# A decode step with cached attention and a gated MLP: whole heads of K and V as 64 KB rows in three slots

## The chip, the cores and the metric

The kernel runs on one core of a Trainium2 chip. The metric is the device time of one execution in microseconds, taken as the median of three runs.

## What is computed

One token (x, 576 wide) goes through a layer norm. Its result xn feeds two branches, and both are added to x:

```python
xn = layernorm(x)
q = (xn @ wq).reshape(32 heads, 128)
scores = einsum("hd,hkd->hk", q, k_cache) * 128**-0.5      # 16384 keys a head
o = einsum("hk,hkd->hd", softmax(scores), v_cache)
h = gelu_tanh(xn @ w_gate) * (xn @ w_up)                   # 4608 wide
out = x + o.reshape(4096) @ wo + h @ w_down
```

All data are float32. The caches hold 32 heads x 16384 x 128 each, 268 MB for K and as much for V. The weights are 9.4 MB (wq, wo) and 10.6 MB (gate, up, down). Everything is read once, so 588 MB cross from HBM into SBUF.

## The kernel before

**Slots.** All large loads go through one pool of five slots of 128 partitions x 32 KB (`SLOTS`, L42, `slot` L58). They are issued by SP, in the order of the program, on one queue; a load waits until the slot it was given is free. A slot is given out as it comes free, not in turn.

**Tiles.** A head has 16384 keys. They are cut into two tiles of 128 partitions x 64 keys (`R = 64`, `C = 2`), so a tile is 4 MB with one contiguous row of 32 KB a partition. There are T = 64 tiles of K and 64 of V. The loop at L254 runs over t: it loads K tile t and V tile t - 3 (`LAG`), computes the scores of K tile t (`qk`) and the weighted sum of V tile t - 3 (`pv`). So softmax of a head lies between them, written out in three parts (`softmax_a`, `_b`, `_c`, L200 to L217) and placed between the blocks by hand.

**Scores.** `qk` (L184) takes 16 keys at a time: VectorE multiplies the block in place by q, which stands in all 128 partitions (L191), then sums ten of the sixteen products (L196), and ScalarE sums the other six by an activation with accumulation (L195).

**PV.** TensorE multiplies four columns of the exponentials with four keys of V, 512 columns at a time (L226), into one of two PSUM banks `PO`. In rows 32q to 32q + 3 of the bank only the four diagonal blocks are wanted. `out_a` (L237) copies the bank to SBUF by ScalarE; `out_b` (L241) picks the diagonal with four matmuls against `sel`; `norm` (L231) sums the exponentials over partitions and inverts; `out_c` (L248) scales and puts the head's 128 outputs in a column of `oall`.

**q.** wq comes in two loads of 2048 columns, 8 KB pieces (L61, L68), with its last 64 rows as a 1 MB load `qt`. At L112 TensorE computes q with xn spread over 128 columns, so that each of the eight results stands in all partitions, 512 columns each, and ScalarE copies it to SBUF.

**Gate and up.** They come in six loads of 1536 columns (6 KB pieces) at t = 1, 3, ..., 11 (`ffn_load` L127), go through TensorE in four column groups (`ffn_mm` L134), are copied by ScalarE (`ffn_copy` L147) and spread over partitions by four small DMAs of POOL (L151). `ffn_act` (L155) computes gelu(gate) x up.

**The end.** After the loop, w_down comes in three loads and wo in loads of 12, 12, 6 and 2 rows a partition. The last of these is cut by partitions into pieces of 8, 4, 2, 1, 112 and 1 (`LAST`, L35). Each row of a weight is two matmuls of 288 columns into `acc` (`add_out`, L294), in four row groups. `oall` is transposed (L315) and its rows are spread by a small DMA into `oT` (L319). Before the last two rows the two upper groups are merged into the lower ones (L337 to L340); the sum with x (L342) and the store (L343) end the kernel.

What a reader may not see from the words is how V's matmul and its column groups are addressed:

```python
for n in range(i * SUB, (i + 1) * SUB, 4):
    k = c * R + n
    q = 32 * (k // 4 % 4)
    nc.tensor.matmul(OP[h][q : q + 4, :], PE_[h][:, k : k + 4], vt[:, n * DH : (n + 4) * DH], ...)
```

The order of the code is not quite the order of execution: a scheduler works at compile time through the program, and on each engine an instruction that it takes to be ready may go ahead of earlier ones that are not. Each engine then runs its list in that fixed order. The memsets of L322 and L336, for instance, run in the first microseconds.

Of the kernel before, what the change touches and what calls it, by code (L numbers as in the profile page):

```python
# [16 lines left out]
R = 64  # L17
C = SK // (P * R)
T = H * C
LAG = 3  # L20
# [3 lines left out]
SLOTS = 5  # L24
DJ = 4
# [4 lines left out]
QS = 2048  # L30
FS = 1536
FQ = FS // 4
FT = FS // P
WO_T = H * DH // P
LAST = (8, 4, 2, 1, 112, 1)  # L35
# [3 lines left out]
def kernel(ctx: ExitStack, tc: tile.TileContext, x, k_cache, v_cache, wq, wo, wg, wu, wd, out):  # L39
# [3 lines left out]
    spool = ctx.enter_context(tc.tile_pool(name="spool", bufs=3))  # L43
    ps_acc = ctx.enter_context(tc.tile_pool(name="ps_acc", bufs=1, space=bass.MemoryType.PSUM))
    ps_big = ctx.enter_context(tc.tile_pool(name="ps_big", bufs=2, space=bass.MemoryType.PSUM))
# [3 lines left out]
    kv = k_cache.rearrange("b h (c p n) d -> (b h c) p (n d)", p=P, n=R)  # L49
    vv = v_cache.rearrange("b h (c p n) d -> (b h c) p (n d)", p=P, n=R)  # L50
    xf = x.rearrange("b s d -> (b s) d")
    of = out.rearrange("b s d -> (b s) d")
    wmain = {n: w[:DM].rearrange("(p j) f -> p j f", j=DJ) for n, w in (("q", wq), ("g", wg), ("u", wu))}
    wqt = wq[DM:].rearrange("d (s f) -> (d s) f", s=2)
    wov = wo.rearrange("(p t) f -> p t f", t=WO_T)
    wdv = wd.rearrange("(s p t) f -> s p t f", p=P, t=FT)
# [4 lines left out]
    def load_w(n, lo, size):  # L61
        t = slot()
        nc.sync.dma_start(t[:, : DJ * size].rearrange("p (j f) -> p j f", j=DJ), wmain[n][:, :, lo : lo + size])  # L63
        return t

    qt = cpool.tile([P, QS], F32, name="qt")
    nc.sync.dma_start(qt, wqt)
    wq_t = [load_w("q", lo, QS) for lo in range(0, H * DH, QS)]  # L68
# [24 lines left out]
    xn = cpool.tile([1, D], F32, name="xn")  # L93
    nc.vector.tensor_scalar(xn, xrow, mv[:, 0:1], rstd, op0=ALU.subtract, op1=ALU.mult)
    px = ps_s.tile([P, 512], F32, tag="sm", name="px")
    xm = xn[:, :DM].rearrange("o (p j) -> o j p", j=DJ)
# [3 lines left out]
    nc.vector.tensor_copy(xd, xn[:, DM:].unsqueeze(2).to_broadcast([1, D - DM, 2]))  # L100
# [3 lines left out]
    xnb = cpool.tile([P, DJ, P], F32, name="xnb")  # L104
    nc.vector.tensor_copy(xnb, xp[:, :DJ].unsqueeze(2).to_broadcast([P, DJ, P]))
    xt = cpool.tile([P, 2], F32, name="xt")
    nc.vector.tensor_scalar(xt, par, xp[:, DJ:], None, op0=ALU.mult)
    xtb = cpool.tile([P, 2, P], F32, name="xtb")
    nc.vector.tensor_copy(xtb, xt.unsqueeze(2).to_broadcast([P, 2, P]))

    Q = {}
    for s, w in enumerate(wq_t):  # L112
        wv = w.rearrange("p (j f) -> p j f", j=DJ)
        for g in range(QS // 512):
            pq = ps_big.tile([P, 512], F32, tag="pb", name="pq")
            for j in range(DJ):
                nc.tensor.matmul(pq, xnb[:, j, :], wv[:, j, g * 512 : (g + 1) * 512], start=j == 0, stop=False)  # L117
            nc.tensor.matmul(pq, xtb[:, s, :], qt[:, g * 512 : (g + 1) * 512], start=False, stop=True)  # L118
            qs = cpool.tile([P, 4, DH], F32, name=f"q{s}{g}")
            nc.scalar.activation(qs.rearrange("p a d -> p (a d)"), pq, AF.Copy)  # L120
            for i in range(4):
                Q[(s * 4 + g) * 4 + i] = qs[:, i : i + 1, :]

    gu = cpool.tile([P, 2, DF // P], F32, name="gu")
    FW = {}

    def ffn_load(which, s):  # L127
        t = FW[which, s] = load_w("gu"[which], s * FS, FS)
        w = (wg, wu)[which]
        src = bass.AP(tensor=w.tensor, offset=w.offset + DM * DF + s * FS,  # L130
                      ap=[[DF, D - DM], [FS // 2, 2], [1, FS // 2]])
        nc.sync.dma_start(t[:, DJ * FS : DJ * FS + FS // 2], src)

    def ffn_mm(which, s):  # L134
        t = FW.pop((which, s))
        pg = ps_big.tile([P, 512], F32, tag="pb", name="pg")
        for j in range(DJ + 1):
            for q in range(4):
                if j < DJ:
                    lhs, rhs = xnb[:, j, :32], t[:, j * FS + q * FQ : j * FS + (q + 1) * FQ]  # L140
                else:
                    o = DJ * FS + (q % 2) * FQ
                    lhs, rhs = xtb[:, q // 2, :32], t[:, o : o + FQ]
                nc.tensor.matmul(pg[32 * q : 32 * q + 32, :FQ], lhs, rhs, start=j == 0, stop=j == DJ)  # L144
        return pg

    def ffn_copy(pg, which, s):  # L147
        gc = spool.tile([P, FQ], F32, name="gc", bufs=1)
        nc.scalar.activation(gc, pg[:, :FQ], AF.Copy)
        for q in range(4):  # L150
            nc.gpsimd.dma_start(gu[32 * q : 32 * q + 32, which, s * FT : (s + 1) * FT], gc[32 * q : 32 * q + 1, :])  # L151

    hT = cpool.tile([P, DF // P], F32, name="hT")

    def ffn_act():  # L155
        g, u = gu[:, 0], gu[:, 1]
        t1 = cpool.tile([P, DF // P], F32, name="t1")
# [3 lines left out]
        th = cpool.tile([P, DF // P], F32, name="th")  # L161
        nc.scalar.activation(th, t1, AF.Tanh, scale=0.7978845608028654)
        t2 = cpool.tile([P, DF // P], F32, name="t2")
        nc.vector.scalar_tensor_tensor(t2, th, 1.0, g, op0=ALU.add, op1=ALU.mult)
# [207 lines left out]
```

## Time and profile before

| what | value |
|---|---|
| median of 3 runs | 1396.49 us (1396.14 to 1397.85) |
| the profiled execution | 1396.48 us, of which its span is 1394.7 us |
| HBM read | 587.60 MB, 421 GB/s over the span |
| K loads | 64 of 4096 KB, 43.0 us from issue to landing (median) |
| V loads | 64 of 4096 KB, 34.6 us |
| DMA packets | 25618, of them 24692 on SP's queue |

The times in the profile are of one execution, measured by the hardware. The busy time of an engine is the sum of its instructions. A line number such as L191 is a line of the kernel before. The chain that ended last is followed back from the last instruction to whatever released each step. The granted clock of TensorE is a share of its full speed.

### The profile page before, as it was taken

The page shows a single profiled execution, that of the slowest core. Times are in us where ns is not written, and L with a number is a line of the kernel's source. Part 1 is how long each engine was busy: PE and PEld are TensorE (multiplying, and loading weights), DVE is VectorE, ACT ScalarE, POOL GpSimd, SP SyncE. Part 2 cuts the span into 40 slices and gives each one's busy share as a digit, 9 for nine tenths or more (in the row PEclk, how much of TensorE's full clock was granted, in tenths as well). Part 3 has the DMA queues.
Part 4 walks back from the last instruction along what each step waited for, and adds up shares of the span by engine and source line. Part 5 has one row for each costly group of instructions (what it writes and reads, how often), then busy time and mean ns, then how long its engine had stood idle before and what let it go on. Part 6 is the DMA issues. An engine that isn't in the chain of part 4 may idle for free.

```text
span 1394.7 us, 10849 instructions
## 1 busy us (share of the span) xinstructions
PE 527.9 (38%) x3071; PEld 151.4 (11%) x3071; DVE 956.3 (69%) x634; ACT 536.1 (38%) x3251; POOL 14.2 (1%) x33
## 2 busy tenths in 40 slices
PE   6634234344234323342243323332333233332575
PEld 3211001011001000000011000100011001100121
DVE  1977565739877877778777877787777777787500
ACT  0644333325443444344344434444434433443300
POOL 0000000000000000000000000000000000000000
PEclk9866667565665665656656566665666666656677
DMA  9999999999999999999999999999999999999993
GB/s 406 422 426 431 422 432 428 419 438 429 428 432 435 425 432 434 429 430 435 431 428 433 430 432 430 432 430 431 432 432 430 430 433 430 431 432 430 430 428 124
DMA packets 25618, 588.36 MB, mean 422 GB/s; under 512 B 3267, under 2 KB 3285, under 8 KB 7254
## 3 DMA queue, kind: packets, MB, share of 16 engines
q1 hardware_dynamic: 24692, 587.61, 98.4%
q8 instruction: 24, 0.39, 0.1%
q14 instruction: 36, 0.29, 0.1%
q0 software_dynamic: 864, 0.06, 0.0%
q10 hardware_dynamic: 2, 0.00, 0.0%
HBM read 587.60 MB, written 0.00 MB: 421 GB/s over the span
## 4 chain that ended last, share of the span: by engine, by line
DMA 72%; DVE 20%; PE 7%; issue 1%; POOL 0%; SPq 0%; ACT 0%; DVEq 0%
DMA slot<-in_A_k_cache_dram 34%; DMA slot<-in_A_v_cache_dram 34%; DVE slot L191 12%; DVE s L196 7%; PE po L226 5%; DMA slot<-in_A_wo_dram 3%; DMA gu<-gc 2%; PE pg L144 1%; PE acc L297 1%; POOL gu L151 0%; PE pt L206 0%; DVE pm L202 0%; PE pb L212 0%; PE pl L233 0%; SPq L63 0%
## 5 line engine op out<-in xcount | busy, mean ns | idle before, releaser
L191 DVE TENSOR_TENSOR slot<-slot,q 128x2048 f32<-128x2048 f32 x256 | 574.5, 2286 | 259.4 <-DMA slot<-in_A_k_cache_dram 259.3
L226 PE MATMUL po<-slot,pe 128*4 128x512 f32 x2048 | 372.0, 893 | 758.1 <-DMA slot<-in_A_v_cache_dram 758.1
L195 ACT ACTIVATE jk<-slot 128x128 f32<-128x128 f32 x1536 | 453.2, 296 | 521.7 <-DVE slot L191 518.5
L196 DVE TENSOR_REDUCE s<-slot 128x10 f32<-128x1280 f32 x256 | 367.7, 1478 | 0.0
L195 ACT ACTIVATION_READ_ACCUMULATOR jk<-slot 128x1 f32 x1536 | 286.8, 187 | 0.0
L226 PEld LDWEIGHTS po<-slot,pe 128*4 128x4 f32 x2048 | 60.2, 111 | 1015.7 <-DMA slot<-in_A_v_cache_dram 749.6
L245 PE MATMUL pc<-sel,o 128*128 128x1 f32 x256 | 35.3, 259 | 39.6 <-ACT o L239 39.6
L239 ACT ACTIVATE o<-po 128x512 f32<-128x512 f32 x32 | 19.0, 595 | 78.5 <-PE po L226 78.5
L214 ACT ACTIVATE nb<-pb 128x1 f32<-128x1 f32 x32 | 5.5, 171 | 95.6 <-PE pb L212 95.6
L337 DVE COPY part<-acc 64x288 f32<-64x288 f32 x1 | 0.5, 461 | 60.7 <-PE acc L297 60.7
L245 PEld LDWEIGHTS pc<-sel,o 128*128 128x128 f32 x256 | 32.6, 199 | 71.2 <-ACT o L239 71.2
L117 PE MATMUL pq<-slot,xnb 128*128 128x512 f32 x64 | 31.6, 641 | 7.9 <-DMA slot<-in_A_wq_dram 7.9
L235 DVE RECIPROCAL rl<-pl 128x1 f32<-128x1 f32 x32 | 5.4, 169 | 38.2 <-PE pl L233 38.2
L210 DVE TENSOR_REDUCE nm<-pt 1x1 f32<-1x128 f32 x32 | 8.9, 278 | 30.3 <-PE pt L206 30.3
L249 ACT ACTIVATE oall<-pc,rl 128x1 f32<-128x1 f32 x32 | 8.4, 261 | 38.2 <-PE pc L245 38.2
L144 PE MATMUL pg<-slot,xnb 128*32 128x384 f32 x192 | 21.0, 588 | 0.9 <-DMA slot<-in_B_w_up_dram 0.6
L120 ACT ACTIVATE q<-pq 128x512 f32<-128x512 f32 x8 | 4.8, 597 | 38.9 <-PE pq L118 38.9
L212 PE MATMUL pb<-nm,ones 1*128 1x1 f32 x64 | 12.0, 255 | 14.6 <-DVE nm L210 14.6
L297 PE MATMUL acc<-slot,oT 128*1 128x288 f32 x128 | 12.9, 559 | 9.8 <-DMA slot<-in_A_wo_dram 9.8
L206 PE MATMUL pt<-ident,pm 128*1 128x128 f32 x32 | 8.9, 280 | 20.0 <-DVE pm L202 19.8
L117 PEld LDWEIGHTS pq<-slot,xnb 128*128 128x128 f32 x64 | 13.2, 208 | 24.5 <-issue 24.5
L297 PE MATMUL acc<-slot,hT 128*1 128x288 f32 x144 | 12.5, 510 | 6.4 <-DMA slot<-in_B_w_down_dram 6.4
(60 smaller groups left out, 131.3 us busy)
## 6 DMA issues: line engine op xcount, KB each, us to landing
slot<-in_A_k_cache_dram SPq DMA_DIRECT2D x64, 4096.0 KB, 43.0
slot<-in_A_v_cache_dram SPq DMA_DIRECT2D x64, 4096.0 KB, 34.6
slot<-in_B_w_down_dram SPq DMA_DIRECT2D x3, 3456.0 KB, 38.0
slot<-in_B_w_gate_dram SPq DMA_DIRECT2D x3, 3072.0 KB, 43.9
slot<-in_B_w_up_dram SPq DMA_DIRECT2D x3, 3072.0 KB
slot<-in_A_wq_dram SPq DMA_DIRECT2D x2, 4096.0 KB, 14.4
slot<-in_A_wo_dram SPq DMA_DIRECT2D x2, 3456.0 KB
slot<-in_A_wo_dram SPq DMA_DIRECT2D x1, 1728.0 KB, 33.4
```

The source lines that it names most:

```text
L117: nc.tensor.matmul(pq, xnb[:, j, :], wv[:, j, g * 512 : (g + 1) * 512], start=j == 0, stop=False)
L144: nc.tensor.matmul(pg[32 * q : 32 * q + 32, :FQ], lhs, rhs, start=j == 0, stop=j == DJ)
L191: nc.vector.tensor_mul(blk, blk, Q[h].to_broadcast([P, SUB, DH]))
L195: nc.scalar.activation(jk, blk[:, n, :], AF.Copy, accum_out=S[h][:, o + n : o + n + 1])
L196: nc.vector.tensor_reduce(S[h][:, o : o + nv], blk[:, :nv, :], axis=AX.X, op=ALU.add)
L206: nc.tensor.transpose(PT[h][:1, :P], PM.pop(h), ident)
L210: nc.vector.tensor_reduce(nm, PT.pop(h)[:1, :P], axis=AX.X, op=ALU.max, negate=True)
L212: nc.tensor.matmul(pb[:, :1], ones[:1, :], nm, start=True, stop=True)
L226: nc.tensor.matmul(OP[h][q : q + 4, :], PE_[h][:, k : k + 4], vt[:, n * DH : (n + 4) * DH], start=k < 16, stop=k >= C * R - 16)
L239: nc.scalar.activation(OS[h], OP.pop(h), AF.Copy)
L245: nc.tensor.matmul(PC[h][:, :1], o4[:, j * DH : (j + 1) * DH], sel[:, j : j + 1], start=j == 0, stop=j == 3)
L297: nc.tensor.matmul(acc[q : q + 1, :HALF], lhs, w[:, i * HALF : (i + 1) * HALF], start=q not in seen, stop=last)
```

## The change

- **Rows and slots.** A tile is now a whole head: 128 partitions x 128 keys, 8 MB, one row of 64 KB a partition (`R = 128`). There are three slots of 64 KB a partition. The loop runs over heads without a lag: load K and V of head h, eight blocks of scores, softmax, PV.
- **Weights first.** wq is one load of 128 rows of 64 KB. Gate and up are loaded whole before the first head: three of their four rows a partition in a slot each, the fourth row and the last 64 weight rows in a slot `mix` that also holds wq's last rows. The copy of gate's and of up's result lies in the same slot as its weights, until four small DMAs of POOL have spread it.
- **q.** It is computed in four column groups with xn spread over 32 columns, one copy of 128 x 1024; a head's q is then spread over the partitions by a matmul against ones, a head ahead (`q_spread`).
- **PV's diagonal.** VectorE multiplies the PSUM bank in place by `sel` and sums the four blocks; TensorE then sums over partitions with one matmul against ones.
- **Normalisation.** The sums of the exponentials are kept for all heads (`lsum`) and summed over partitions, inverted and multiplied in at the end.
- **The end.** w_down comes as 28 and 8 rows a partition, wo as 20, 6, 3, 2 and 1 rows, all over 128 partitions; the merge comes before row 26.

The core of the diff:

```diff
-R = 64
+R = SK // P
-SLOTS = 5
+SLOTS = 3
-LAST = (8, 4, 2, 1, 112, 1)
+WD_PIECES = (28, 8)
+WO_PIECES = (20, 6, 3, 2, 1)
+MERGE = 26
...
-    kv = k_cache.rearrange("b h (c p n) d -> (b h c) p (n d)", p=P, n=R)
+    kv = k_cache.rearrange("b h (p n) d -> (b h) p (n d)", p=P)
...
+    mix, wq_t = slot(), slot()
...
+    tails = {"q": part_of_mix(wtail["q"])}
+    load(wq_t, wmain["q"])
+    row3 = {}
+    for n in "gu":
+        row3[n] = part_of_mix(wmain[n][:, ROW3:])
+        tails[n] = part_of_mix(wtail[n])
...
+    def q_spread(h):
+        r = 32 * (h // (H // 4))
+        lo = h % (H // 4) * DH
+        pq = ps_s.tile([P, 512], F32, tag="sm", name="pq")
+        nc.tensor.matmul(pq[:, :DH], ones[r : r + 1, :], qrow[r : r + 1, lo : lo + DH], start=True, stop=True)
+        Q[h] = spool.tile([P, 1, DH], F32, name="qs")
+        nc.scalar.activation(Q[h][:, 0, :], pq[:, :DH], AF.Copy)
...
+    def ffn(which):
+        n = "gu"[which]
+        t = slot()
+        w = load(t[:, :ROW3], wmain[n][:, :ROW3])
+        gc = t[:, ROW3 : ROW3 + FG]
+        steps = [(3, row3[n]), (DJ, tails[n])] + [(j, w[:, j * DF : (j + 1) * DF]) for j in range(3)]
+        pg = project(steps, FG, FB)
+        nc.scalar.activation(gc.rearrange("p (b f) -> p b f", f=FB), pg, AF.Copy)
         for q in range(4):
-            nc.gpsimd.dma_start(gu[32 * q : 32 * q + 32, which, s * FT : (s + 1) * FT], gc[32 * q : 32 * q + 1, :])
+            nc.gpsimd.dma_start(gu[32 * q : 32 * q + 32, which, :], gc[32 * q : 32 * q + 1, :])
...
     def out_a(h):
-        OS[h] = spool.tile([P, 512], F32, name="o4", bufs=1)
-        nc.scalar.activation(OS[h], OP.pop(h), AF.Copy)
+        o4 = PO[h % 2].rearrange("p (r d) -> p r d", d=DH)
+        nc.vector.tensor_mul(o4, o4, sel.unsqueeze(2).to_broadcast([P, 4, DH]))
+        OM[h] = spool.tile([P, DH], F32, name="om")
+        nc.vector.tensor_reduce(OM[h], o4.rearrange("p r d -> p d r"), axis=AX.X, op=ALU.add)
...
+    q_spread(0)
+    for h in range(H):
+        KT[h] = load(slot(), kv[h])
+        VT[h] = load(slot(), vv[h])
         for i in range(NSUB):
+            qk(h, i)
+            if h == 0 and i == 3:
+                ffn_act()
+            if h > 0 and i == 3:
+                out_a(h - 1)
+                out_b(h - 1)
+        KT.pop(h)
+        softmax(h)
+        if h + 1 < H:
+            q_spread(h + 1)
+        pv(h)
...
+    out_a(H - 1)
+    out_b(H - 1)
+    for j, w in enumerate(wd_rows):
+        add_out(j % 2, hT[:, j : j + 1], w)
+
+    pl = ps_s.tile([P, 512], F32, tag="sm", name="pl")
+    nc.tensor.matmul(pl[:, :H], ones, lsum, start=True, stop=True)
+    rl = cpool.tile([P, H], F32, name="rl")
+    nc.vector.reciprocal(rl, pl[:, :H])
+    on = cpool.tile([P, H], F32, name="on")
+    nc.vector.tensor_mul(on, oall, rl)
     po = ps_s.tile([P, 512], F32, tag="sm", name="pot")
-    nc.tensor.transpose(po[:H, :P], oall, ident)
+    nc.tensor.transpose(po[:H, :P], on, ident)
```

`project` runs a list of weight rows through TensorE, for each row two or three blocks of columns in four column groups. `part_of_mix` loads a piece into the next free columns of `mix`.

More of the change, by code (lines that the diff above doesn't have):

```diff
@@ L59, in slot, with load @@
         return slots.tile([P, R * DH], F32, tag="s", name="slot")
[L61 to L68, printed above, removed]
+    def load(dst, src):
+        nc.sync.dma_start(dst, src)
+        return dst
+    mix, wq_t = slot(), slot()
@@ L124 @@
[L124 to L145, printed above, removed]
@@ L299, in add_out @@
             seen.add(q)
[L301 to L312 removed]
+    wd0, wd1, wo1 = slot(), slot(), slot()
@@ new lines @@
+    a, b = WD_PIECES
+    n0 = WO_PIECES[0]
+    load(wd0[:, : a * D], wdv[:, : a * D])
+    load(wd1[:, : b * D], wdv[:, a * D :])
+    load(wd1[:, b * D : (b + n0) * D], wov[:, : n0 * D])
+    lo = n0
+    for n in WO_PIECES[1:]:
+        load(wo1[:, (lo - n0) * D : (lo + n - n0) * D], wov[:, lo * D : (lo + n) * D])
+        lo += n
+    wd_rows = [wd0[:, j * D : (j + 1) * D] for j in range(a)] + [wd1[:, j * D : (j + 1) * D] for j in range(b)]
+    wo_rows = [wd1[:, (b + j) * D : (b + j + 1) * D] for j in range(n0)]
```

245 lines of the change are left out of this document (87 added, 158 removed).

## The prediction

> **What bounds the kernel now.** First the page: where the engines are busy, then what the DMA queues did, then the chain that ended last.
>
> ```profile
> PE 527.9 (38%) x3071; PEld 151.4 (11%) x3071; DVE 956.3 (69%) x634; ACT 536.1 (38%) x3251; POOL 14.2 (1%) x33
> ...
> GB/s 406 422 426 431 422 432 428 419 438 429 428 432 435 425 432 434 429 430 435 431 428 433 430 432 430 432 430 431 432 432 430 430 433 430 431 432 430 430 428 124
> DMA packets 25618, 588.36 MB, mean 422 GB/s; under 512 B 3267, under 2 KB 3285, under 8 KB 7254
> ...
> q1 hardware_dynamic: 24692, 587.61, 98.4%
> ...
> DMA 72%; DVE 20%; PE 7%; issue 1%; POOL 0%; SPq 0%; ACT 0%; DVEq 0%
> ```
>
> No engine is over 69%; the one queue that SP feeds keeps the sixteen DMA engines 98.4% busy, and 72% of the chain is DMA. The rate is flat but for the last slice. So I read the rate by stage (columns: stretch, its length, busy time and count of PE, PEld, DVE, ACT, POOL, then granted clock, DMA share, GB/s).
>
> ```profile
> 10.00:20.00 10.00, 4.23 (x5) 1.85 (x6) 0.00 (x0) 0.00 (x0) 0.00 (x0) 1.00 1.01 424
> 2.00:100.00 98.00, 55.45 (x194) 23.63 (x198) 63.26 (x53) 37.69 (x210) 3.10 (x6) 0.81 1.00 424
> 100.00:350.00 250.00, 96.84 (x597) 27.73 (x589) 161.87 (x107) 91.38 (x554) 9.79 (x20) 0.65 1.01 429
> 350.00:700.00 350.00, 116.06 (x669) 30.75 (x673) 265.24 (x171) 146.32 (x901) 0.00 (x0) 0.64 1.00 431
> 1050.00:1364.00 314.00, 123.06 (x750) 32.55 (x750) 202.01 (x131) 114.05 (x692) 0.56 (x1) 0.65 1.00 431
> 1364.00:1368.00 4.00, 3.09 (x48) 1.14 (x48) 0.00 (x0) 0.00 (x0) 0.00 (x0) 1.00 0.96 312
> 1368.00:1372.00 4.00, 0.00 (x0) 0.00 (x0) 0.00 (x0) 0.00 (x0) 0.00 (x0) 0.71 0.57 209
> 1376.00:1380.00 4.00, 4.00 (x36) 1.19 (x32) 0.00 (x0) 0.00 (x0) 0.00 (x0) 0.51 0.06 28
> 1384.00:1388.00 4.00, 4.00 (x48) 1.52 (x44) 0.00 (x0) 0.00 (x0) 0.00 (x0) 0.66 0.08 28
> 1388.00:1392.00 4.00, 2.86 (x36) 0.79 (x24) 0.91 (x2) 0.00 (x0) 0.00 (x0) 1.00 0.00 1
> ```
>
> From 350 us to 1364 us the DMA share is 1.00 at 431 GB/s: nothing but fewer or cheaper packets can shorten that stretch. The last rows say more. After 1372 us the share is 0.06, which is 1/16: **one engine** works alone at 28 GB/s for some 15 us. The kernel ends when this late engine ends, not when the average one does. Is its lateness made by the eight-four-two-one-row cuts of the last load? The chain of waits and the issues on SP's queue answer that (start, length, what).
>
> ```profile
> 1346.43 36.53 DMA slot<-in_A_wo_dram
> 1383.00 6.28 PE acc L297 x72
> 1389.30 0.47 DVE part L337
> 1390.47 0.99 PE acc L297 x8
> 1391.49 0.45 DVE x L342
> ...
> 1361.01 3.83 SPq L305 DMA_DIRECT2D slot<-in_A_wo_dram  x5
> ```
>
> The load issued at 1346.43 lands only at 1383.00, and the cut pieces were issued behind it, at 1361.01 and after. So the engine was already late before the cuts: every engine carries the same bytes, one of them loses time along the way, and the end is its end. I take this lag as unchanged: every engine still carries a sixteenth of the same bytes, and the work of the other engines beside it hardly changes.
>
> The profiled execution took 1396.48 us, 1.8 us more than its span, and stands at the median of the runs (1396.49). A change under 0.2% (2.8 us) counts as none, about what a measurement of this kernel can tell.
>
> **What the change takes off the DMA.** *K and V.* Rows of 8 KB (wq, 10 to 20 us) ran at 424 GB/s, rows of 32 KB at 431. Per engine that is 8192 x 16 / 424 = 309.1 ns and 32768 x 16 / 431 = 1216.4 ns a row, so a byte costs 0.0369 ns and a row 6.7 ns beside its bytes. A head's K and V now take one row of 64 KB a partition: 8192 rows fewer, 512 an engine, 512 x 6.7 ns = **3.4 us less**. Bounds: no gain, if a row goes out in two pieces; and a loss of 20.6 us, if long rows run at the 424 of the slowest steady row (536.9 MB at 424 instead of 431). I take 3.4, since the 32 KB rows are nearest.
>
> The Trainium skill speaks against it: "DMA: Bandwidth & Descriptors", section "Latency and other measured facts", has copies slowed by row pitches at large powers of two (207 GB/s at 512 KiB, 164 at 2 MiB). By it a doubled pitch could cost rate; no run here shows that so far, and what it would cost by this trace is the first rival below.
>
> *wq, gate, up.* wq goes from 8 KB to 64 KB rows, gate and up from 6 KB to 54 KB and 18 KB. Against 431, the first 98 us lost 98 x 7/431 = 1.6 us and the next 250 us 250 x 2/431 = 1.2 us, and these hold all loads of small rows: **2.8 us less** (bounds 0 and 2.8). *The last rows.* The cuts give the lowest engines a row of the 8, 4 and 2 pieces besides 7 of the 112, ten rows for eight; without them 2 x 4.6 KB at 28 GB/s, **0.3 us less** (0 to 0.5). Together 6.5.
>
> **What hides beside the DMA.** Durations from the groups (busy, mean ns of one):
>
> ```profile
> L191 DVE TENSOR_TENSOR slot<-slot,q 128x2048 f32<-128x2048 f32 x256 | 574.5, 2286 | 259.4 <-DMA slot<-in_A_k_cache_dram 259.3
> L195 ACT ACTIVATE jk<-slot 128x128 f32<-128x128 f32 x1536 | 453.2, 296 | 521.7 <-DVE slot L191 518.5
> L196 DVE TENSOR_REDUCE s<-slot 128x10 f32<-128x1280 f32 x256 | 367.7, 1478 | 0.0
> L245 PE MATMUL pc<-sel,o 128*128 128x1 f32 x256 | 35.3, 259 | 39.6 <-ACT o L239 39.6
> L239 ACT ACTIVATE o<-po 128x512 f32<-128x512 f32 x32 | 19.0, 595 | 78.5 <-PE po L226 78.5
> L337 DVE COPY part<-acc 64x288 f32<-64x288 f32 x1 | 0.5, 461 | 60.7 <-PE acc L297 60.7
> L202 DVE TENSOR_REDUCE pm<-s 128x1 f32<-128x128 f32 x32 | 9.2, 286 | 3.3
> ```
>
> PV of a half head, and SP's own longest wait, stand in the timeline and in the waits of SP's queue:
>
> ```profile
> 1339.78 6.57 PE L226 MATMUL po<-slot,pe 128*4 128x512 f32 x32 [3.40 <-DMA slot<-in_A_v_cache_dram]
> SPq L182 <- DVE s L196: 947.0, 52, 28.1
> ```
>
> A head's K and V are 2 x 8.39 MB, 38.9 us at 431. DVE needs 8 x (2.286 + 1.478) = 30.1 us, two softmax reductions 0.6, and the new masked product and sum. No row shows them: from L337, 288 columns out of PSUM in 0.461, 512 columns lie between 0.46 and 0.82; I take 0.8 twice, 1.6. With about 0.7 us of waiting for PE in the softmax that is 33.0: 5.9 us to spare. **The slots** follow from it. V of the next head takes the slot of this K, free some 32 us after K landed, while the next K is still landing until 38.9. The next K but one takes V's slot, free after softmax and PV, at 33 + 2 x 6.57 = 46, needed at 58. So the queue always holds a load; the cover is 7 us where five slots of half the size gave far more. SP already waits so for a K slot (947.0 us in 52 times), with transfers under way. Behind each such wait stand all later loads, so if the cover goes, each head pays: 32 x what is missing.
>
> q spread adds two matmuls and a copy a head, out_b has two matmuls instead of eight of 0.259, and ACT's copy of 0.595 goes. All lie beside the DMA: nothing. Uncovered they would save more than they cost.
>
> **What it adds at the start.** wq (1.05 + 8.39 MB) has landed by about 24 us, row 3 and tails of gate and up by 41, gate's first three rows (7.08 MB) by 57, up's, in wq's slot, by 74. Then K of head 0 needs a slot: the mixed one, or gate's, which now waits until the row in it has been spread to partitions by POOL.
>
> ```profile
> 235.36 3.47 PE pg L144 x40
> 238.85 0.50 ACT gc L149
> 239.63 1.32 POOL gu L151 x3
> 241.09 12.07 DMA gu<-gc
> 285.43 6.22 PE pg L144 x40
> ```
>
> 40 matmuls took 3.47 to 6.22 us by clock; the last 72 for gate then take 6 to 11, to some 66, the copy of three times the width to 67.5, POOL to 69.5. The mixed slot is free after up's 48 first matmuls, 4 to 7.5 us, at 72 to 75: hole 0 to 3. Gate's slot would be free after the small DMAs, 12.07 us beside 32 KB packets. With 12.07 again it is free at 81.5, a hole of 8. But the big queue runs dry at 74, and then nothing is in the way of the small ones; I estimate a hole of about 4 by this. I take **2 us more** (0 to 8), as either slot can come first.
>
> **What it adds at the end.** The end after the last landing (about 1389) was 5.7 us: merge, two rows, sum, store. One row at the end instead of two changes little. But the normalisation moved from each head to the end: sum over partitions, reciprocal, product, transpose, and then the small DMA into oT.
>
> ```profile
> 1364.55 3.09 PE L297 MATMUL acc<-slot,hT 128*1 128x288 f32 x48 [3.61 <-DMA slot<-in_B_w_down_dram]
> 1374.86 5.57 PE L297 MATMUL acc<-slot,oT 128*1 128x288 f32 x48 [7.21 <-DMA slot<-in_A_wo_dram]
> ...
> oT<-orow POOLq DMA_DIRECT2D x1, 16.0 KB, 6.4
> ```
>
> Count from the landing of the last K. Softmax ends at 33 us, PV (64 matmuls, 13 us at the low clock, 10 if PE warms up underway as in the 72 above) at 43. The DMA ends at 66: V 19.5, then 36 rows of w_down and 32 of wo, each 0.295 MB and 0.68 us. If PE does w_down first, 36 rows at 3.09/12 = 0.26, that is 52.5; normalisation 1.5 and DMA 6.4 or a little more give oT at 61, while wo's first 20 rows landed at 58. PE restarts at the low clock (5.57 for 12 rows), 20 rows at 0.26 and the merge of 1.2 follow: 73, seven after the DMA, where it was 2.5 before: 4.5 more. If the transpose comes ahead of w_down, oT is there by 53: nothing more. I take **2 us more** (0 to 4.5), short of the middle.
>
> **The sum.** 1396.5 - 3.4 - 2.8 - 0.3 + 2 + 2 = **1394.0**, just short of what counts as faster (1393.7). Own range of this case: best 1396.5 - 6.5 = 1390.0, worst, with 4 each at start and end, 1398.
>
> **Rivals.** *Long rows are read slower* (the other side). Place: every K and V load. Price: 20.6 us at 424 GB/s, so 1396.5 + 20.6 - 3.1 + 4 = 1418. It turns the sign by more than 0.2% (over 1399.3) once K and V take 5.3 us over the forecast's 1242.2, a rate under 430. For it: 424 for wq, whose partitions also lie 64 KB apart. Against it: those pieces were 8 KB, and the rate rises from 8 KB to 32 KB rows. [...]
>
> *The first hole and the end eat the gain.* If the hole is 8, the end costs 4.5 and the 64 KB rows bring nothing: 1396.5 - 3.1 + 12.5 = 1406; with 6 less of that, 1400.
>
> *Three slots starve.* If DVE or PV runs past the 7 us of cover, DVE becomes the bound: 1.3 us a head would be 42 us, 1435. Against it stand the 5.9 us above.
>
> *The late engine catches up.* If its lag comes from how loads queue rather than from its own work, 8 to 15 us at the end go: 1379 to 1386. Against it: 1383.00 above.
>
> **How the numbers follow.** Forecast 0.61 (faster 0.29, same 0.30, slower 0.02); eaten gain 0.15 (same 0.03, slower 0.12); slow rows 0.10 and starving 0.06, all slower; catching up 0.08, faster. Faster 0.37, same 0.33, slower 0.30. The range 1386 to 1408 leaves out catching up (0.08), starving (0.06) and half of the slow rows (0.05), 0.2 in all.
>
> **What would show it.** K and V stretches at 432 GB/s or a little over; at 429 or less the row rival holds. DMA share below 1.00 only near 74 us, for 0 to 4 us. DVE waiting for K in every head by about 6 us; if SP's wait for a slot is followed by DMA idling, the slots starve. At the end a few us at a share of 0.06 still, though fewer, since a fast engine can now run only one load ahead. PE's last wo rows before or after the last landing tell the place of the transpose. The prediction is wrong if the lag changes size, or if PE's order differs at the start.

## The result, and the profile after

The changed kernel takes **1481.16 us** (median of four runs, 1480.83 to 1481.66) against 1396.32 us for the kernel before: 1.0606 times as long, with a 95% interval of 1.0587 to 1.0624. It is 6% slower. The forecast of 1394.0 us and its range up to 1408 both missed it; the case that comes nearest is the one called "Three slots starve", at half the price that was paid.

The page of the changed kernel, in the lines that answer to those of before: busy times, rate in 40 slices, SP's queue, and the shares of the chain that ended last.

```profile
PE 402.3 (27%) x2881; PEld 107.0 (7%) x2881; DVE 990.4 (67%) x668; ACT 656.9 (44%) x3240; POOL 6.4 (0%) x17
...
GB/s 405 426 398 426 422 399 399 415 392 412 371 398 397 397 398 424 399 394 401 396 371 397 424 427 370 398 397 396 399 398 397 425 396 398 386 385 419 373 386 300
...
q1 hardware_dynamic: 11380, 587.60, 93.4%
...
DVE 55%; PE 24%; ACT 12%; DMA 6%; issue 3%; POOL 0%; ACTq 0%; SPq 0%; DVEq 0%
```

DMA fell from 72% of the chain to 6%, DVE rose from 20% to 55% and PE from 7% to 24%. Yet DVE is busy for only 67% of the span, less than before. An engine that leads the chain while a third of its time is idle may be waiting inside a ring: it waits for somebody who waits for it. The windows of the middle (columns as in the prediction) show what the transfers lose.

```profile
350.00:700.00 350.00, 90.33 (x618) 22.46 (x610) 253.79 (x166) 166.82 (x830) 0.00 (x0) 0.62 0.94 401
700.00:1050.00 350.00, 85.17 (x568) 20.90 (x568) 258.29 (x168) 170.35 (x848) 0.00 (x0) 0.60 0.94 399
```

The share is 0.94 where it was 1.00. Both stretches are even: the loss is not one hole, every head pays. The groups say where DVE stands still (mean ns of one, then idle time ahead and its releaser).

```profile
L196 DVE TENSOR_TENSOR slot<-slot,qs 128x2048 f32<-128x2048 f32 x256 | 573.9, 2283 | 0.0
...
L225 DVE TENSOR_TENSOR po<-po,sel 128x512 f32<-128x512 f32 x32 | 22.4, 700 | 339.8 <-PE po L220 339.8
...
L227 DVE TENSOR_REDUCE om<-po 128x128 f32<-128x512 f32 x32 | 22.1, 692 | 1.1
```

Before, DVE's idle time stood ahead of the scores and ended with a landing of K (259.3 us). Now there is none ahead of the scores. 339.8 us, 10.6 a head, stand ahead of the new mask at L225, and PV on PE ends them. DVE's timeline over one head, with PV from PE's, shows the ring (start, length, engine, line, idle before).

```profile
565.60 0.70 DVE L225 TENSOR_TENSOR po<-po,sel 128x512 f32<-128x512 f32 x1 [9.93 <-PE po L220]
566.34 0.69 DVE L227 TENSOR_REDUCE om<-po 128x128 f32<-128x512 f32 x1
566.94 4.48 DVE L196 TENSOR_TENSOR slot<-slot,qs 128x2048 f32<-128x2048 f32 x2
...
592.91 2.87 DVE L200 TENSOR_REDUCE s<-slot 128x10 f32<-128x1280 f32 x2
596.09 0.28 DVE L204 TENSOR_REDUCE pm<-s 128x1 f32<-128x128 f32 x1 [0.31 <-ACT jk L199]
596.84 0.28 DVE L208 TENSOR_REDUCE nm<-pt 1x1 f32<-1x128 f32 x1 [0.46 <-PE pt L206]
608.50 0.70 DVE L225 TENSOR_TENSOR po<-po,sel 128x512 f32<-128x512 f32 x1 [11.38 <-PE po L220]
```

```profile
598.60 9.82 PE L220 MATMUL po<-slot,pe 128*4 128x512 f32 x64 [0.54 <-ACT pe L214]
```

Read the order, not only the times. After softmax (596.84) the next thing on DVE's list is L225, the mask of the head just scored. The code writes it behind the fourth block of the **next** head; the compile-time order has put it ahead of the first. DVE runs its list in order, so the scores of the next head wait for PV, though their K is there: by the landing records the K scored from 609.85 on landed at 597.0, 12.8 us earlier. One turn is mask and sum 1.3, scores 28.8 (566.94 to 595.78), softmax 2.8 up to PV's start, PV 9.8: 42.9 us from 565.60 to 608.50. It is the longest of three turns that repeat (42.9, 41.9 and 41.5 from mask to mask). A head's K and V need 38.9.

The mean turn comes from the chain, which runs through every PV: between the two rows below lie 17 heads.

```profile
724.90 9.88 PE po L220 x64
...
1441.35 10.05 PE po L220 x64
1454.67 16.64 PE acc L256 x248
```

(1441.35 - 724.90) / 17 = 42.1 us a head. DVE's timeline has the last thing ahead of the first scores:

```profile
103.73 0.20 DVE L179 SCALAR_TENSOR_TENSOR hT<-t,gu 128x36 f32<-128x36 f32 x1 [25.97 <-DMA gu<-slot]
```

From 103.9 on, 32 turns of 42.1 end at 1451, where the last PV does (1451.4); the weights' matmuls and the end take 27.5 more. That gives the span of 1478.9 to within half a microsecond.

### The profile page after: what moved, and what is told of

It is laid out like the page before. It is cut to its first block, busy times and chain, and to the rows that moved or that the text cites. A ratio compares the mean times of both kernels' runs of the same rounds, so it can differ in the third digit from the quotient of the medians.

```text
span 1478.9 us, 10328 instructions
## 1 busy us (share of the span) xinstructions
PE 402.3 (27%) x2881; PEld 107.0 (7%) x2881; DVE 990.4 (67%) x668; ACT 656.9 (44%) x3240; POOL 6.4 (0%) x17
## 4 chain that ended last, share of the span: by engine, by line
DVE 55%; PE 24%; ACT 12%; DMA 6%; issue 3%; POOL 0%; ACTq 0%; SPq 0%; DVEq 0%
DVE slot L196 34%; PE po L220 20%; DVE s L200 18%; ACT jk L199 10%; DMA slot<-in_B_w_up_dram 3%; DMA slot<-in_A_wq_dram 2%; DVE po L225 2%; PE acc L256 1%; DMA gu<-slot 1%; PE pg L132 1%; ACT pe L214 1%; PE pb L210 1%; PE pt L206 1%; DVE pm L204 1%; DVE nm L208 1%
## 5 line engine op out<-in xcount | busy, mean ns | idle before, releaser
L199 ACT ACTIVATE jk<-slot 128x128 f32<-128x128 f32 x1536 | 475.3, 309 | 312.5 <-DVE slot L196 268.2
L196 DVE TENSOR_TENSOR slot<-slot,qs 128x2048 f32<-128x2048 f32 x256 | 573.9, 2283 | 0.0
L220 PE MATMUL po<-slot,pe 128*4 128x512 f32 x2048 | 289.9, 730 | 14.8 <-ACT pe L214 14.5
L225 DVE TENSOR_TENSOR po<-po,sel 128x512 f32<-128x512 f32 x32 | 22.4, 700 | 339.8 <-PE po L220 339.8
L132 PE MATMUL pg<-slot,xnb 128*32 128x384 f32 (+1 forms) x256 | 29.1, 613 | 36.5 <-DMA slot<-in_B_w_gate_dram 18.7
L231 PE MATMUL pc<-ones,om 128*128 128x1 f32 x64 | 12.2, 260 | 49.8 <-DVE om L227 49.8
L147 PE MATMUL pq<-qrow,ones 1*128 1x128 f32 x64 | 24.8, 488 | 0.0
L227 DVE TENSOR_REDUCE om<-po 128x128 f32<-128x512 f32 x32 | 22.1, 692 | 1.1
L210 PEld LDWEIGHTS pb<-nm,ones 1*128 1x128 f32 x64 | 15.8, 305 | 23.2 <-issue 22.5
L147 PEld LDWEIGHTS pq<-qrow,ones 1*128 1x128 f32 x64 | 16.0, 307 | 0.6 <-issue 0.6
## 6 DMA issues: line engine op xcount, KB each, us to landing
slot<-in_B_w_gate_dram SPq DMA_DIRECT2D x1, 2304.0 KB, 28.8
```

The lines of the kernel that those rows point to most:

```text
L132: nc.tensor.matmul(pg[32 * q : 32 * q + 32, b, :size], lhs, rhs[:, lo : lo + size], start=k == 0, stop=k == len(steps) - 1)
L147: nc.tensor.matmul(pq[:, :DH], ones[r : r + 1, :], qrow[r : r + 1, lo : lo + DH], start=True, stop=True)
L196: nc.vector.tensor_mul(blk, blk, Q[h].to_broadcast([P, SUB, DH]))
L199: nc.scalar.activation(jk, blk[:, n, :], AF.Copy, accum_out=S[h][:, lo + n : lo + n + 1])
L210: nc.tensor.matmul(pb[:, :1], ones[:1, :], nm, start=True, stop=True)
L220: nc.tensor.matmul(PO[h % 2][q : q + 4, :], pe[:, k : k + 4], vt[:, k * DH : (k + 4) * DH], start=k < 16, stop=k >= R - 16)
```

## The experiments

**Out_a held behind the fourth block.** The same kernel, with the mask where the code writes it.

```diff
-        nc.vector.tensor_reduce(S[h][:, lo : lo + nv], blk[:, :nv, :], axis=AX.X, op=ALU.add)
+        return nc.vector.tensor_reduce(S[h][:, lo : lo + nv], blk[:, :nv, :], axis=AX.X, op=ALU.add)
...
-            qk(h, i)
+            last = qk(h, i)
...
-                out_a(h - 1)
+                with tc.issue_after(last.ins):
+                    out_a(h - 1)
```

> The changed kernel, with the masked product of a finished head held on VectorE's list until the fourth block of scores of the next head has been issued, which is where the code writes it. Theory (order): the 339.8 us of VectorE's waiting for PV at the masked product close a ring of scores, softmax, PV, mask of 42.0 us a head; without that wait VectorE needs 31.4 us a head, less than the 38.7 us of DMA, and the time falls from 1481 to 1388 us, 1383 to 1394, with the late DMA engine back at the end. Rival (three slots are too few by themselves): the queue still runs dry in every head, DMA share stays near 0.94 and the time stays over 1430. Rival (the weights at the start and the late end cost most): only part comes back, over 1405.

Measured 1395.97 us, 0.9997 (0.9989 to 1.0006) of the kernel before. Groups and windows of this run:

```profile
L196 DVE TENSOR_TENSOR slot<-slot,qs 128x2048 f32<-128x2048 f32 x256 | 576.5, 2283 | 211.8 <-DMA slot<-in_A_k_cache_dram 210.2
```

```profile
350.00:700.00 350.00, 97.56 (x639) 25.63 (x639) 271.73 (x177) 178.27 (x892) 0.00 (x0) 0.61 1.00 429
700.00:1050.00 350.00, 97.65 (x639) 25.27 (x639) 271.23 (x179) 179.05 (x896) 0.00 (x0) 0.61 1.00 426
```

DVE waits for K again, the share is 1.00 again, and 85 us are gone. Nothing was taken out; the mask and its sum, two instructions a head, changed their place. The time lies 2 us above the range expected (1383 to 1394), 8 us above the 1388 it was built on: the rate stayed at 426 to 429 GB/s instead of rising over 431. That is taken up with the late engine below.

**The line moved in the code, nothing held.** Is it the place in the code that counts?

```diff
-            if h > 0 and i == 3:
+            if h > 0 and i == 6:
```

> The kernel after, with out_a and out_b of the last head written behind the seventh block of scores instead of the fourth, and nothing held. Theory (the place in the code doesn't set the place on VectorE's list; the compile-time order does, and puts out_a ahead of the next head's first block wherever it is written): VectorE waits for PV as before, a head takes 42 us, 1481 us (1478 to 1484). Rival (the place in the code counts): 1396, as with out_a held behind the fourth block.

A single run: 1481.46 us.

```profile
L225 DVE TENSOR_TENSOR po<-po,sel 128x512 f32<-128x512 f32 x32 | 22.4, 700 | 339.6 <-PE po L220 339.6
```

The same wait to 0.2 us. Three blocks later in the code changes nothing, because the order on the engine is not the order of the code. Why the compile-time order prefers the mask was not tried and stays open; perhaps it counts K as landing later than PV ends.

**The ring made longer.** If the ring sets the time, more work for DVE inside it must cost its full length: thirteen of sixteen products are summed by DVE instead of ten.

```diff
-N_ACT = 6
+N_ACT = 3
```

> The changed kernel with three of sixteen sums on ScalarE instead of six, and nothing else: VectorE sums 13 in place of 10 and so takes 0.44 us more in seven of a head's eight blocks (in the last, ScalarE's six sums of about 0.43 us each ended after VectorE's, so 0.7 us goes there). Theory (a ring of scores, softmax, PV and mask sets each head's 42.0 us): every us put on VectorE is paid in full, 2.4 us a head, 77 us, 1558 us, 1545 to 1595. Rival (DMA, or its late engine, is still the bound in the changed kernel): fewer instruction loads, so some 8 us faster, 1473, or no change.

Measured 1567.13 us, 1.1222 (1.1207 to 1.1237) of before.

```profile
L200 DVE TENSOR_REDUCE s<-slot 128x13 f32<-128x1664 f32 x256 | 470.2, 1879 | 0.0
...
L225 DVE TENSOR_TENSOR po<-po,sel 128x512 f32<-128x512 f32 x32 | 22.4, 700 | 331.2 <-PE po L220 331.2
```

The sum grew from 1.478 to 1.879 us, 0.40 x 8 blocks x 32 heads = 103 us; the time grew by 86, 9 more than expected. Most of the rest is the 0.31 us that DVE waited for ScalarE in each softmax (row 596.09 above), now gone, and 0.27 a head less waiting for PV (339.8 to 331.2). That wait hardly shrank, as it must in a ring. The same edit in a kernel bound by DMA makes it faster (below).

**The mask given back to ScalarE and PE.** One part of the change undone: the bank is copied by ScalarE and the diagonal picked by four matmuls, as before. To make room for the copy, three small tiles of gate and up share one buffer, and the exponentials have one buffer instead of two.

```diff
-        nc.vector.tensor_mul(o4, o4, sel.unsqueeze(2).to_broadcast([P, 4, DH]))
-        OM[h] = spool.tile([P, DH], F32, name="om")
-        nc.vector.tensor_reduce(OM[h], o4.rearrange("p r d -> p d r"), axis=AX.X, op=ALU.add)
+        OM[h] = spool.tile([P, 512], F32, name="o4", bufs=1)
+        nc.scalar.activation(OM[h], PO[h % 2], AF.Copy)
...
-        nc.tensor.matmul(pc[:, :1], OM.pop(h), ones[:, :1], start=True, stop=True)
+        for j in range(4):
+            nc.tensor.matmul(pc[:, :1], o4[:, j * DH : (j + 1) * DH], sel[:, j : j + 1], ...)
```

> The kernel after with the diagonal of PV picked as in the kernel before: ScalarE copies the bank, TensorE picks with four matmuls; all else stays but two small buffers shared to make room for the copy. Theory (the part that costs is the one instruction on VectorE's list that waits for PV): now ScalarE waits for PV at the head's start, 10 us, then has 0.6 + 20.3 us of work; the ring PV 9.8, copy 0.6, sums 20.3, softmax 2.8 is 33.5 us, under the 38.7 of the DMA. So the time is that of the kernel with out_a held, 1396 us (1393 to 1399). Rival (three slots with whole heads starve whatever waits, since K's slot is freed late): over 1410. Rival (the 64 KB rows or the weights first cost time themselves): 1400 to 1410.

Measured 1395.33 us, 0.9993 (0.9983 to 1.0002).

```profile
L194 DVE TENSOR_TENSOR slot<-slot,qs 128x2048 f32<-128x2048 f32 x256 | 574.1, 2284 | 278.7 <-DMA slot<-in_A_k_cache_dram 278.7
...
L223 ACT ACTIVATE o<-po 128x512 f32<-128x512 f32 x32 | 19.1, 597 | 292.6 <-PE po L218 292.6
```

This is the instructive one. ScalarE now stands 292.6 us in the very same wait, just as early on its list, and it costs nothing: its work of 20.3 us a head leaves room for 10 us of waiting, DVE's 33 does not.

**The mask alone in the kernel before.** VectorE masks the diagonal, five slots and the rest stay.

```diff
-        nc.scalar.activation(OS[h], OP.pop(h), AF.Copy)
+        o4 = OP.pop(h).rearrange("p (r d) -> p r d", d=DH)
+        nc.vector.tensor_mul(o4, o4, sel.unsqueeze(2).to_broadcast([P, 4, DH]))
+        OS[h] = spool.tile([P, DH], F32, name="om")
+        nc.vector.tensor_reduce(OS[h], o4.rearrange("p r d -> p d r"), axis=AX.X, op=ALU.add)
```

> The kernel before with one part of the change alone: the diagonal of PV masked and summed on VectorE instead of copied by ScalarE and picked by four matmuls. There the finished head lies three tiles back, so VectorE finds PV done. Theory (place, not price): the two instructions of 0.70 and 0.69 us cost 44 us of VectorE's time in all, beside the DMA, and the time stays at 1396 within 2 us. Rival (the masked product itself is the price): 1396 + 44 = 1440, or at least 10 us more than before.

Measured 1396.19 us, 0.9998 (0.9989 to 1.0007). The operations are free where the transfers cover them; the price was their place in a ring, not their work.

**Rows of 32 KB again.** The held kernel, with each K and V loaded as two halves of 32 KB rows.

```diff
-        KT[h] = load(slot(), kv[h])
-        VT[h] = load(slot(), vv[h])
+        KT[h], VT[h] = slot(), slot()
+        for dst, view in ((KT[h], kv), (VT[h], vv)):
+            for c in range(2):
+                load(dst[:, c * R * DH // 2 : (c + 1) * R * DH // 2], view[2 * h + c])
```

> As e1_hold, but each K and V load is cut in two loads of 32 KB rows into the two halves of its slot. Theory (a row costs 6.7 ns beside its bytes): 512 rows more an engine, so 3.4 us slower than e1_hold; by the median packet of the changed kernel (2418 ns for 64 KB against twice 1216) up to 7 us slower. Rival (row length is worth nothing): equal to e1_hold within 1 us. Rival (long rows are read slower): faster than e1_hold. A first half that lands earlier also lets the scores start earlier, which is worth nothing while DMA is the bound.

Measured 1399.3 us (1.002, 1.0011 to 1.0029), 3.3 us more than the held kernel. Two windows of this run:

```profile
700.00:1050.00 350.00, 96.79 (x637) 24.81 (x637) 270.94 (x177) 179.54 (x898) 0.00 (x0) 0.61 1.00 431
...
1380.00:1392.00 12.00, 9.98 (x114) 3.40 (x116) 0.46 (x1) 0.00 (x0) 0.00 (x0) 0.74 0.06 21
```

The 3.3 us aren't the price of the rows alone. One engine works alone at the end again, as before the change, so wo's first 20 rows landed only at 1381.3 and PE had its work on wo still to do: from the last row's landing to the end of the span it takes 8.7 us, against 6.5 in the held kernel. The two profiled executions lie 5.2 us apart, 3.0 of it up to that landing and 2.2 behind it. So the 64 KB rows bring 3.3 us at most; their own share was not separated, and the number of loads changed with them.

**Whose engine is late?** The prediction took the late engine's lag as given. The packet records show two small traffics beside the data, both of them instruction loads: 8 KB packets on queue q14 and 16 KB packets on q8. In the kernel before, the last of the sixteen engines falls back in steps, most of them of 0.66 to 0.71 us, and no more steps than q14 has packets. Below is, for some loads, about when the first engine has finished its part, how far the last and the 15th lie behind it, and q14's 8 KB packets up to the load's landing (counted with those ahead of the span):

```
                  first     last   15th   packets
before            53.6      0.45   0.43   6
                  359.0     5.10   2.35   16
                  718.5    10.48   3.24   25
                  1068.1   16.02   5.30   36
                  1337.0   19.81   6.32   42
before, N_ACT 2   718.4     4.30   3.52   16
                  1337.0    8.64   6.46   26
after, held       643.6     6.43   3.26   21
                  1195.6    5.91   3.36   36
                  1382.0    5.15   2.60   41
```

If ScalarE's instructions are most of these loads, fewer of them should help the kernel before.

```diff
-N_ACT = 6
+N_ACT = 2
```

> The kernel before with two of sixteen sums on ScalarE instead of six, so 1024 activations with accumulation fewer; VectorE sums fourteen in place of ten, 0.59 us more in each of 256 blocks, 151 us, and stays under the DMA. Theory (the late engine): the DMA engine that ends some 15 us after the others loses its time to the loading of ScalarE's instructions, 0.68 us for each 8 KB of them; with a third of these activations some 16 of about 26 such loads go, 11 us, and the time falls to 1385, 1382 to 1389. Rival (the engine is slow by itself, or late by the cuts of the last load): 1396 as before. Rival (VectorE is in the way): slower than before.

Measured 1385.5 us, 0.9921 (0.9907 to 0.9934). The rows of q14 in the pages of before and of this run (packets, MB, share):

```profile
q14 instruction: 36, 0.29, 0.1%
```

```profile
q14 instruction: 20, 0.16, 0.0%
```

16 packets fewer at 0.67 us are 10.7 us; 10.8 were measured. That these packets are ScalarE's follows from the counts: 2048 of its instructions fewer are 16 packets fewer, 128 a packet; q8 stayed at 24 packets. With no sums on ScalarE at all:

```diff
-N_ACT = 6
+N_ACT = 0
```

> The kernel before with all sums on VectorE, none on ScalarE: 2.3 us for sixteen in place of 1.48, VectorE about 88% busy. Theory (late engine): the rest of ScalarE's instruction loads goes, some 9 of 0.68 us, but the next engine is then as late as this one, so of the 10 to 11 us that two of sixteen gave only 2 to 3 more: 1383, 1381 to 1385. Rival (VectorE becomes the bound): over 1386.

Measured 1385.3 us, 0.9922 (0.9908 to 0.9935), 0.3 us above the range expected (1381 to 1385): 11 packets, and no gain over 20. The lag did fall further, from 8.5 to 5.1 us at 1329 us, with the 15th engine at 3.5. But between 325 and 350 us the rate is 386 GB/s at a share of 0.93, where the run with two sums on ScalarE has 430 at 1.00, and VectorE is busy for 23.9 of these 25 us. That hole is worth 2.6 us, as much as was to be gained. So the rival is at least part of it: VectorE, with all sums, comes near the bound. Whether the next engine takes over the end was not separated from that.

In the held kernel the lag stays near 5 to 6 us, and still nothing is gained. A reading that fits: the scores of a head start, and its K's slot comes free, only after the last engine's part has landed; VectorE has some 6.6 us a head to spare (211.8 / 32), and once the lag has used that up, a fast engine has no next load to go on with and waits for the late one. So the lost time is paid on the way, as 426 to 429 instead of 431 GB/s from 350 to 1300 us, and not at the end. These windows lost (350 x 2 + 350 x 5 + 250 x 3) / 431 = 7.4 us, most of the 8 us of the first experiment. Three slots alone don't set it: with rows of 32 KB, where scores can start on half a head, the lag grew to 14.8 us in the same three slots, at 431 GB/s, and showed at the end. The held kernel with fewer sums on ScalarE tests whether the packets are what is paid for:

```diff
-N_ACT = 6
+N_ACT = 3
```

> The same edit in e1_hold, where the mask no longer waits. Theory (there DMA is the bound, and the engine that loads ScalarE's instructions is its slowest): VectorE needs 34.5 us a head, still under 38.7; half of the sums' instructions go, some 12 loads of 8 KB at 0.68 us, so 8 us faster than e1_hold: 1388, 1385 to 1391. Rival (the cover of three slots is too thin): VectorE's 3 us more a head hold the loads back, 1396 or more.

Measured 1385.96 us, 0.9926 (0.9913 to 0.9938): 10.0 us less, for 12 packets fewer (8 us by 0.67 each, so close and not exact; its five runs spread over 3.5 us). The rate is 430 to 431 GB/s again from 350 to 1300 us.

**The hole at the start.** In the changed kernel, in the held one and in this last one alike the queue runs half empty at 70 to 80 us; the windows of the changed kernel:

```profile
70.00:75.00 5.00, 3.39 (x44) 1.15 (x36) 0.00 (x0) 0.56 (x1) 1.68 (x4) 1.00 0.47 195
75.00:80.00 5.00, 4.18 (x52) 1.72 (x56) 0.77 (x4) 0.23 (x1) 0.00 (x0) 1.00 0.62 210
```

K of head 0 waits there for the small DMAs that read gate's result out of gate's slot; against 431 this is 2.7 + 2.6 = 5.3 us. Gate's result was put into up's slot, so that gate's comes free earlier:

```diff
+    tg, tu = slot(), slot()
+    load(tg[:, :ROW3], wmain["g"][:, :ROW3])
+    load(tu[:, :ROW3], wmain["u"][:, :ROW3])
...
-        gc = t[:, ROW3 : ROW3 + FG]
+        gc = tu[:, ROW3 + which * FG : ROW3 + (which + 1) * FG]
```

> As e7_nact3, with the copy of gate's result put beside up's weights, so that gate's slot is free as soon as its matmuls have run and K of head 0 need not wait for the small DMAs. Theory (the hole of 70 to 80 us costs what it lasts): 4 to 5 us faster than e7_nact3, 1383. Rival (the DMA time that the hole costs is won back behind it, since something else sets the pace): equal to e7_nact3 within 1 us.

A miss: 1397.14 us (1.0004, 0.9995 to 1.0013), 11 us **more** than without the edit. The windows of this run show the hole gone and a larger one opened; VectorE's timeline and then ScalarE's say by what. The last fence has the same two rows of ScalarE without the edit.

```profile
70.00:75.00 5.00, 2.51 (x32) 0.78 (x24) 0.00 (x0) 0.00 (x0) 0.81 (x2) 1.00 0.92 389
...
110.00:120.00 10.00, 0.00 (x0) 0.00 (x0) 5.29 (x4) 1.74 (x9) 0.00 (x0) 0.50 0.77 302
...
130.00:140.00 10.00, 0.00 (x0) 0.00 (x0) 10.00 (x6) 2.41 (x12) 0.00 (x0) 0.50 0.48 210
140.00:150.00 10.00, 2.04 (x9) 1.11 (x13) 7.72 (x7) 3.40 (x16) 0.00 (x0) 0.50 0.31 106
```

```profile
114.71 0.20 DVE L182 SCALAR_TENSOR_TENSOR hT<-t,gu 128x36 f32<-128x36 f32 x1 [23.15 <-DMA gu<-slot]
114.84 4.49 DVE L199 TENSOR_TENSOR slot<-slot,qs 128x2048 f32<-128x2048 f32 x2
```

```profile
91.10 0.23 ACT L179 ACTIVATE th<-t 128x36 f32<-128x36 f32 x1 [21.42 <-DVE t L177]
91.24 1.11 ACT L163 ACTIVATE slot<-pg 128x1152 f32<-128x1152 f32 x1
```

```profile
77.39 0.23 ACT L176 ACTIVATE th<-t 128x36 f32<-128x36 f32 x1 [7.95 <-DVE t L174]
83.86 1.13 ACT L160 ACTIVATE slot<-pg 128x1152 f32<-128x1152 f32 x1 [6.24 <-PE pg L132]
```

It is the same fault twice more, on two engines. The activation of gate and up is written behind head 0's fourth block; the compile-time order has put it first. On ScalarE the tanh waits for gate's small DMAs, which now run beside K's 64 KB packets, and up's result, ready on PE at 83.5, is copied behind it at 91.2 instead of 83.9 as without the edit. So up's small DMAs start late, VectorE's last step in that activation waits for them until 114.7 (106.1 without the edit), the scores of head 0 stand behind that step, and V of head 1 gets K's slot only 32 us later still. So this activation was held too, until the fourth block of head 1, first without and then with the move of gate's result:

```diff
-            if h == 0 and i == 3:
-                ffn_act()
             if h > 0 and i == 3:
                 with tc.issue_after(last.ins):
                     out_a(h - 1)
+                    if h == 1:
+                        ffn_act()
```

> The kernel with out_a held and thirteen sums on VectorE (1386.0 us), and with the activation of gate and up held until block 3 of head 1; gate's copy stays in gate's slot. Theory: VectorE starts on head 0 when its K lands, some 97 us, instead of 106.1; the hole of 2.8 + 1.0 us at 130 to 150 us goes, the one of 5.3 us at 70 to 80 us stays: 1382 us, range 1380 to 1384.5. Rival A (the small DMAs hold the slots): nothing, 1385.5 to 1386.5. Rival B (the late engine takes it): 1385 to 1386.

Measured 1383.95 us, 0.9917 (0.9903 to 0.9930), 2.0 us less than before the hold where 4 were expected, inside the range given. By the time alone this is not clear: the two intervals overlap, and two of the five runs lie at 1385.8 and 1386.3, where both rivals are. The trace is: VectorE starts when K lands (98.7 instead of 106.2 us), and the rate at 130 to 150 us rises from 309 and 389 to 415 and 420 GB/s.

> The kernel with gate's copied result in up's slot (1397.1 us), and with the activation of gate and up held on VectorE's list until block 3 of head 1. Theory: in that kernel VectorE stood still from 91.4 to 114.7 us at the activation's last step, which waits for the small DMAs of up, while K of head 0 had long landed; so K's slot came free at 147 instead of about 122, and the queue lost 5.1 + 7.5 us at 130 to 150 us (210 and 106 GB/s against 431). With VectorE free at K's landing these 12.6 us go: 1384.5 us, or 1380 if counted from the kernel with the copy in each matrix's own slot (1386.0 less its 9 us of holes, plus the 3 us at 110 to 120 us that stay, since the third load still waits for the small DMAs). Range 1379 to 1387. Rival A, the small DMAs themselves hold the slots: the hole stays and the time is 1395 to 1398. Rival B, the late engine takes what the queue gains: 1388 to 1393.

Measured **1380.24 us**, 0.9882 (0.9869 to 0.9896), the fastest kernel of this study and 1.2% faster than the one before. VectorE's first scores and the same windows in this run:

```profile
95.49 4.49 DVE L199 TENSOR_TENSOR slot<-slot,qs 128x2048 f32<-128x2048 f32 x2 [87.16 <-DMA slot<-in_A_k_cache_dram]
```

```profile
70.00:75.00 5.00, 2.18 (x28) 0.65 (x20) 0.00 (x0) 0.00 (x0) 0.47 (x1) 1.00 0.89 376
...
130.00:140.00 10.00, 8.45 (x65) 1.63 (x64) 5.95 (x3) 3.98 (x16) 0.00 (x0) 0.79 0.97 415
140.00:150.00 10.00, 0.00 (x0) 0.00 (x0) 10.00 (x6) 2.41 (x12) 0.00 (x0) 0.73 0.97 419
```

DVE starts when K lands, and both holes are gone. The move that cost 11 us by itself brings 3.7 once the wait behind it is out of the way.

## Why the prediction was wrong

**The step that failed** is "What hides beside the DMA", in its sum of DVE's head and in "V's slot, free after softmax and PV, at 33 + 2 x 6.57 = 46, needed at 58". It counted DVE's work a head as 33.0 us and laid PV beside it, with the mask where the code writes it. The length came out: 42.9 less PV's 9.8 is 33.1. That is partly luck, since its terms differ: the scores took 28.8 and not 30.1, the mask 1.3 and not 1.6, and from the last score to PV's start it takes 2.8, some of it on PE and ScalarE, and not 1.3. But the mask stood ahead of the next scores, PV came in series, and 33.1 + 9.8 = 42.9 left no cover against 38.9. The change had added a wait of DVE for PE, and the place of that wait on DVE's list was taken from the code, although the text ahead of the prediction says that the order of the code is not the order of execution. Both ends were at hand in the rows: 33 with the mask late, 43 with it first by the prediction's own 10 us for PV, which is 4 us a head, 131 us in all (46 by its 13). The range held only the first. That 85 came, and not 131 or more, is because the turns took 42.1 on average (102 us over 38.9), and part of the weights at the end came in beside the last of them.

The rival "Three slots starve" named the outcome, "DVE becomes the bound", and its condition, "if DVE or PV runs past the 7 us of cover", but not the mechanism: the held kernel and the one with the mask given back have the same three slots and don't starve. Its price of 1.3 us a head was an assumption; 42.1 - 38.9 = 3.2 were measured. Its chance of 0.06 rested on the 5.9 us of cover that the same step had worked out, so it could not warn of an error in that step.

The other terms can be judged on the held kernel, 1396.0 where the sum gave 1394.0:

- *64 KB rows*: 3.4 less taken; 3.3 at most by the run with 32 KB rows, and not separated from its longer end. The rival "Long rows are read slower" falls: the held kernel read at 432 GB/s from 100 to 350 us, the run with 32 KB rows at 431. The Trainium skill ("DMA: Bandwidth & Descriptors", section "Latency and other measured facts") gives its slow power-of-two pitches for tiles of 16 KiB rows cut out of wider ones, at 512 KiB and more, and names contiguous tiles as a way out. Here a load is contiguous with either row length, so the prediction's use of that rule reached too far, and no run here tests it.
- *wq, gate, up*: by the packet records the weights ran at 431 GB/s from 5 to 65 us, against 426 before. By 70 us that put them 0.33 MB ahead, 0.8 us; the rest of the 2.8 us wasn't measured by itself.
- *The mask*: 0.8 us twice taken, 0.70 and 0.69 measured.
- *The start*: 2 us taken within 0 to 8; 5.3 by the two windows, and 3.7 in the time once the hole was taken out. The big queue running dry did not make the small DMAs quick enough.
- *The end*: 2 us taken within 0 to 4.5; by the packet records it takes 6.5 us from the last row's landing to the end of the span, against 6.4 before. Nothing was added in the held kernel; in the changed kernel itself it is 9.1 us.
- *The late engine*: "I take this lag as unchanged" was wrong, it fell from 20 us to 5 (to under 4 in the changed kernel, where DMA is not the bound). The rival "catches up" was right on that and wrong on the gain of 8 to 15 us: by the reading above the late engine still carries its bytes and its interruptions, and the time follows those, wherever the waiting shows.

With DVE's order as written the forecast would have been right to 0.2%. Some of that is luck: what the start cost beyond its term, the end did not cost.

## What to carry to other kernels

When a change makes an engine wait for another, look up where that instruction stands on the engine's list, not in the code, and price both places: with two engines in series in every turn, their sum is compared with the transfer, not the longer one. Such a ring shows as an engine that leads the chain while idle for a third of its time, with most of its idle time ahead of one cheap instruction; here moving that instruction, or giving the wait to an engine with room for it, was worth more than any work saved. And when an edit that should remove a hole makes things worse, look for the next wait of the same kind before dropping it.

## What the runs showed of the hardware

Instruction loads are small, and still seem to cost data transfers time. In the kernel before, the last engine fell back in steps of mostly 0.66 to 0.71 us as q14's packets came, and with 16 packets fewer (0.13 MB) the kernel was 10.8 us faster, 0.8%, though the share of q14 on the page is 0.1% against 0.0%. That the steps are caused by those packets, and not by something else that goes with ScalarE's instructions, is the reading that fits the counts; the packets weren't changed alone. Their own records last 0.31 us in most cases, less than half a step, and what makes up the rest isn't shown. Small DMAs beside 64 KB packets are slow: gate's four of 4.5 KB a row, issued from 68.7 on, released ScalarE's tanh only at 91.1 with K of head 0 beside them; issued from 68.5 on with the queue half empty, they released it at 77.4.
